# Float64 weights rebuilt as float32: which engine does which part of the bit work

## Chip, cores and metric

The kernel runs on one core of one Trainium2 chip. The metric is the device time of one execution in microseconds, median over runs. Times of single instructions, stages and waits come from one profiled execution.

## What is computed

Pooled attention over 4 batches and 8 heads (sequence 1152, head size 64), and behind it a rational MLP over the 2304 pooled rows. Cut to what matters:

```python
q_pool = q.reshape(B, H, S // 2, 2, D).mean(axis=3)
scores = q_pool @ k.transpose(0, 1, 3, 2) / np.sqrt(D)
attn = softmax(scores)                      # [4, 8, 576, 1152]
x = (attn @ v).transpose(0, 2, 1, 3).reshape(2304, 512)
h = x @ w_in                                # w_in [512, 2048], float64
P = a[0] + a[1]*h + a[2]*h**2 + a[3]*h**3
Q = 1 + abs(b[0])*abs(h) + abs(b[1])*h**2
out = (P / (Q + 1e-6)) @ w_out              # w_out [2048, 512], float64
```

The two weight matrices arrive as 64-bit floats. The chip's engines work on 32 bits, so the kernel has to make a float32 out of the two 32-bit words of every weight before it can use it.

## The kernel before

**Attention.** A unit is one batch and two heads. Preparing a unit loads k, q and v, pools q, takes a scale from sums of squares (ACT, L606), splits each operand in a high and a low float16 part (ACT L660 to L667, DVE L673 to L678), and turns k and q by transposing DMAs on SP's queue (L687). There are 144 attention tiles. A tile makes a first score product into the PSUM tile `sc` (L718), a row maximum on DVE (L725), a turn of it by a small matmul (L728) and a copy of that row by ACT (L732), a second score product into `st` (L741, L742), the exponential on ACT (L749) and a split of its result on DVE (L757). Products with v follow (L771), with a copy out by ACT (L788).

**MLP.** 18 chunks of 128 rows, 4 steps each. A step multiplies with `wi` (48 matmuls, L913) into one PSUM tile `ph`, runs a chain over ACT (L926, L931, L952, L956), DVE (L935, L939, L963, L967, L975) and POOL (L944, L948, L971), and multiplies with `wo` (12 matmuls, L984 to L986).

**Weights.** `wi` and `wo` are converted once, each in 16 pieces of 128 x 512 weights, in `weights` (L1092). A piece is loaded by SP (L457) into `raw`, which has two buffers and holds the low and the high word of each weight side by side, so that an engine that reads one of the words reads every second 32-bit word. `w_win` (L461) lets POOL read the high words as float32 and multiply them by 2^-111 into `wf`, which moves the exponent into the place it needs. `w_bits` (L467) is three DVE instructions: the top three bits of the low word are brought into the freed low half of the high word (L471, on 16-bit pieces), everything but the sign is cleared in the high word (L472), and `wf` is shifted left by 3 and joined with both by a bitwise or (L473). ACT then takes a sum of squares of the piece (`w_stat`, L478). When all 16 pieces are there, a scale is formed, ACT writes the high float16 part (L500) and DVE the low one (L504). For `wi`, column sums follow (L509 on ACT, L514, L517). `wo` uses the same `wf` buffer, so its first piece waits for the last low part of `wi`. The MLP's own tiles are opened by `w_close` (L524) once both weights are split: the first MLP step stands behind the last L504.

**What sets the order.** Each engine runs its instructions in a fixed order. `Plan` (L35) computes it when the kernel is built: every piece of work is added with an engine, a duration in ns and a due time, the planner goes forward and backward over them, and the earliest plan's order is written out for all engines. Those durations stand in the `add` calls (L1096 to L1099 for the weights); changing one can move any instruction of the program. At run time an instruction at the head of an engine's queue that waits holds all behind it on that engine.

## Time and profile before

| | |
|---|---|
| median of 3 runs | 953.59 us (952.13 to 958.34) |
| the profiled execution | 954.2 us, of which its span is 952.4 us |
| PE, DVE, ACT, POOL busy | 816.0, 794.1, 602.2, 446.0 us |
| first row maximum (L725) starts | 31.4 us |
| weight pieces of `wi`: first to last L473 starts | 12.7 to 113.1 us |
| weight pieces of `wo`: first to last L473 starts | 149.7 to 207.8 us |
| first MLP matmul (L913) | 232.7 us |
| PE busy up to 230 us, and behind it | 122.9 us of 230, 693.1 us of 722.4 |

How to read it: a busy share over the whole span mixes two stages. Up to 230 us there is attention and weight conversion and no MLP; behind it attention and MLP run side by side. A row of a group of instructions gives the line, the engine, what is written and read, the count, the busy time, the mean duration, and the idle time of the engine just before them with what ended it. The stretches table gives for each engine its busy time in a stretch, with the instruction count in brackets, and then the granted TensorE clock and the DMA share.

### The profile page before, as it was taken

The numbers are of one execution on the slowest core, as the hardware profiler recorded it, in microseconds if no ns is written. First come the engines' busy times: TensorE is split into PE (matmuls) and PEld (weight loads), VectorE is DVE, ScalarE is ACT, GpSimd is POOL, SyncE is SP. The second block draws the span as 40 slices with busy tenths as digits, with TensorE's granted clock in tenths as the row PEclk, the third lists the DMA queues.
The fourth block names the chain that finished last, engine by engine and source line by source line (L and its number), as shares of the span: only waits on it lengthen the run. The fifth ranks groups of instructions, "written<-read, shape, count | busy, mean of one in ns | idle before, by whom it ended". The sixth has DMA issues, their size and how long they took to land.

```text
span 952.4 us, 27847 instructions
## 1 busy us (share of the span) xinstructions
PE 816.0 (86%) x12196; PEld 650.4 (68%) x12196; DVE 794.1 (83%) x1075; ACT 602.2 (63%) x905; POOL 446.0 (47%) x482
## 2 busy tenths in 40 slices
PE   0477675545999999989998999989899998999998
PEld 0266554444877877768777788668677777887764
DVE  7698797888999897868999888869888897996765
ACT  4466595456876676657675686557667755775453
POOL 4212103342565553436764553425856544645765
PEclk9998777766999999979999999989999999999999
DMA  5784518462340060652150061445736120430100
GB/s 188 199 182 132 139 35 215 155 177 60 60 103 13 13 149 13 139 124 49 24 140 23 13 150 21 130 117 138 141 125 149 38 40 24 113 113 13 35 12 23
DMA packets 121338, 88.79 MB, mean 93 GB/s; under 512 B 96769, under 2 KB 98817, under 8 KB 121217
## 3 DMA queue, kind: packets, MB, share of 16 engines
q1 hardware_dynamic: 121216, 87.02, 37.0%
q8 instruction: 95, 1.56, 0.7%
q14 instruction: 27, 0.21, 0.1%
HBM read 49.24 MB, written 8.87 MB: 61 GB/s over the span
## 4 chain that ended last, share of the span: by engine, by line
PE 55%; DVE 12%; ACT 6%; POOL 6%; DMA 5%; issue 3%; SPq 1%; POOLq 0%; DVEq 0%; ACTq 0%
PE ph_h L913 15%; PE po L984 5%; PE po L986 5%; PE po L985 5%; PE st L741 5%; PE st L742 5%; PE sc L718 5%; PE sc L771 5%; PE st L771 4%; DVE mt L725 2%; DMA raw_wo<-in_moe_w_out_dram 2%; POOL e L944 1%; DMA k<-spk 1%; POOL e L948 1%; DVE E L757 1%
## 5 line engine op out<-in xcount | busy, mean ns | idle before, releaser
L749 ACT ACTIVATE E<-st,esc 128x1152 int32<-128x1152 f32 x144 | 188.6, 1310 | 92.4 <-PE st L728 63.0
L725 DVE TENSOR_REDUCE mt<-sc 128x1 f16<-128x1152 f32 x144 | 194.5, 1351 | 27.0 <-PE sc L718 18.9
L741 PE MATMUL st<-q,k 128*128 128x128 f16 (+1 forms) x1440 | 182.2, 224 | 34.9 <-ACT q L732 30.2
L913 PEld LDWEIGHTS <-wi 128*128 128x128 f16 x3456 | 199.9, 99 | 16.4 <-DVE t L939 9.3
L913 PE MATMUL ph_h<-x,wi 128*128 128x128 f16 x3312 | 201.9, 221 | 5.7 <-DVE t L939 5.7
L742 PE MATMUL st<-q,kb 65*128 65x128 f16 (+1 forms) x1440 | 182.7, 224 | 2.8 <-DMA kb<-k 2.8
L742 PEld LDWEIGHTS <-kb 65*128 65x128 f16 x1440 | 139.2, 103 | 49.0 <-issue 42.3
L971 POOL TENSOR_TENSOR e<-t,e 128x512 f32<-128x512 f32 x72 | 106.4, 1478 | 118.3 <-DVE e L967 108.4
L771 PEld LDWEIGHTS <-E 128*128 128x128 f16 (+1 forms) x4320 | 152.4, 105 | 12.9 <-issue 6.9
L757 DVE TENSOR_SCALAR E<-E 128x2304 f16<-128x2304 uint16 x144 | 129.8, 908 | 29.8 <-ACT E L749 29.6
L741 PEld LDWEIGHTS <-k 128*128 128x128 f16 x1440 | 139.7, 103 | 14.0 <-issue 8.8
L718 PE MATMUL sc<-k,q 128*128 128x384 f16 (+1 forms) x480 | 104.2, 354 | 42.3 <-DVE mt L725 25.6
L944 POOL TENSOR_SCALAR e<-A,b_abs 128x512 f32<-128x512 f32 x72 | 72.5, 1008 | 97.0 <-ACT A L926 97.0
L984 PE MATMUL po<-wo,g 128*128 128x512 f16 x288 | 109.2, 379 | 0.0
L986 PE MATMUL po<-wo,g 128*128 128x512 f16 x288 | 109.1, 379 | 0.0
L985 PE MATMUL po<-wo,g 128*128 128x512 f16 x288 | 109.1, 379 | 0.0
L948 POOL TENSOR_TENSOR e<-e,A 128x512 f32<-128x512 f32 x72 | 97.7, 1357 | 5.7
L718 PEld LDWEIGHTS <-q 128*128 128x128 f16 (+1 forms) x480 | 39.2, 104 | 69.2 <-issue 33.4
L952 ACT ACTIVATE A<-e,q_one 128x512 f32<-128x512 f32 x72 | 51.9, 721 | 51.7 <-POOL e L948 50.8
L926 ACT ACTIVATE A<-ph_h,cf 128x512 f32<-128x512 f32 x69 | 47.3, 686 | 58.2 <-PE ph_h L913 57.7
L975 DVE SCALAR_TENSOR_TENSOR g<-e,cf,A 128x512 f16<-128x512 f32 x72 | 63.0, 875 | 21.8 <-POOL e L971 21.7
L771 PE MATMUL sc<-v,E 128*128 128x65 f16 (+3 forms) x2160 | 80.3, 201 | 1.1 <-DVE mt L725 1.1
(126 smaller groups left out, 1212.6 us busy)
## 6 DMA issues: line engine op xcount, KB each, us to landing
kn<-in_k_dram SPq DMA_DIRECT2D x16, 576.0 KB, 4.2
vn<-in_v_dram SPq DMA_DIRECT2D x16, 576.0 KB, 5.4
qn<-in_q_dram SPq DMA_DIRECT2D x16, 512.0 KB, 4.9
raw_wi<-in_moe_w_in_dram SPq DMA_DIRECT2D x16, 512.0 KB, 5.3
raw_wo<-in_moe_w_out_dram SPq DMA_DIRECT2D x16, 512.0 KB, 3.6
kb<-k SPq DMA_DIRECT2D x18, 288.0 KB, 4.7
out_dram<-ob SPq DMA_DIRECT2D x16, 256.0 KB, 2.3
keep<-v SPq DMA_DIRECT2D x4, 292.5 KB, 6.2
```

The source lines that it names most:

```text
L718: nc.tensor.matmul(SC[ps, jj, 0:TH], d["q"][:, slot, ps], d["k"][:, h * KC + 3 * jj:h * KC + 3 * jj + 3, :].rearrange("p c m -> p (c m)"), ...
L725: nc.vector.tensor_reduce(mts[t % NM][:, D:D + 1], SC[:, :, 0:TH], AX.XY, ALU.max, negate=True)
L741: nc.tensor.matmul(o, d["k"][:, h * KC + c, :], d["q"][:, slot, qs], start=True, stop=False)
L742: nc.tensor.matmul(o, d["kb"][0:D + 1, h * KC + c, :], d["q"][0:D + 1, KC + slot, qs], start=False, stop=True)
L749: nc.scalar.activation(out=d["e"].rearrange("p (a c) -> p a c", a=3), in_=ST[:, :, 0:TH], func=AF.Exp, bias=esc[:, 1:2], scale=esc[:, 0:1],)
L757: nc.vector.tensor_scalar(e.bitcast(F16), e.bitcast(U16), 2.0 ** -6, None, ALU.mult)
L771: nc.tensor.matmul(pv[:, 0:w], e[:, c, qs, part], pairs[j][n_v][:, h * KC + c, :], start=(c == 0 and i == 0), stop=(c == KC - 1 and i == 2),)
L913: nc.tensor.matmul(mo[c, f]["p2"][:, i, :], wi[wl][:, kk, fs], x[:, xl * KD + kk, :], start=(n == 0), stop=(n == 3 * KD - 1))
L948: nc.gpsimd.tensor_tensor(w["e2"], w["e2"], w["A"], ALU.mult)
L984: nc.tensor.matmul(po, g[0][:, e, :], wo[0][:, kk, :], start=(kk == 0), stop=False)
L985: nc.tensor.matmul(po, g[0][:, e, :], wo[1][:, kk, :], start=False, stop=False)
L986: nc.tensor.matmul(po, g[1][:, e, :], wo[0][:, kk, :], start=False, stop=(kk == KF - 1))
```

## The change

`w_win` moves from POOL to ACT as a parametric relu with scale 2^-111 and a slope of -2^32 for negative inputs: a negative weight comes out positive with an exponent raised by 32, and that bit is the one that lands in the sign's place after the shift by 3. A new `w_low` lets POOL read the low words as 32-bit unsigned integers, multiply them by 2^-29 and 7.49/8 and write the result back as an integer from 0 to 7: these are the top three bits. `w_bits` keeps only the DVE instruction that shifts and joins, now with the low word. In the planner's table POOL's 700 becomes ACT's 630, POOL gets 830 for `w_low`, and DVE's 2300 becomes 800. Behind the changed lines, line numbers are higher by two.

```diff
     def w_win(n, i):
...
-        u = st["raw", n, i][:, :, 1]
-        nc.gpsimd.tensor_scalar(st["wf", n][:, i, :], u.bitcast(F32), 2.0 ** -111, 1.0, ALU.mult, ALU.mult)
+        u = st["raw", n, i][:, :, 1].bitcast(F32)
+        nc.scalar.activation(out=st["wf", n][:, i, :], in_=u, func=AF.Prelu, scale=2.0 ** -111, alpha=-(2.0 ** 32))
+
+    def w_low(n, i):
+        u = st["raw", n, i][:, :, 0].bitcast(U32)
+        nc.gpsimd.tensor_scalar(u, u, 2.0 ** -29, 7.49 / 8, ALU.mult, ALU.mult)

     def w_bits(n, i):
         mi = st["wf", n][:, i, :].bitcast(I32)
-        r = st["raw", n, i]
-        h = r.rearrange("p f w -> p (f w)").bitcast(U16).rearrange("p (f w) -> p f w", w=4)
-        nc.vector.tensor_scalar(h[:, :, 2], h[:, :, 1], 13, None, ALU.logical_shift_right)
-        nc.vector.tensor_scalar(h[:, :, 3], h[:, :, 3], 0x8000, None, ALU.bitwise_and)
-        nc.vector.scalar_tensor_tensor(mi, mi, 3, r[:, :, 1], ALU.logical_shift_left, ALU.bitwise_or)
+        nc.vector.scalar_tensor_tensor(mi, mi, 3, st["raw", n, i][:, :, 0], ALU.logical_shift_left, ALU.bitwise_or)
...
-            add("pool", 700, s + 4, lambda i=i: w_win(n, i), r=[raw], w=[wf], seq=["win"])
-            add("dve", 2300, s + 4, lambda i=i: w_bits(n, i), w=[wf, raw])
+            add("act", 630, s + 4, lambda i=i: w_win(n, i), r=[raw], w=[wf], seq=["win"])
+            add("pool", 830, s + 4, lambda i=i: w_low(n, i), w=[(*raw, "low")], r=[raw], seq=["low"])
+            add("dve", 800, s + 4, lambda i=i: w_bits(n, i), r=[raw, (*raw, "low")], w=[wf])
```

The planner's new order moves instructions on all engines. Three places matter below.

DVE near the start of the program, before the change: the bit work of the second and third piece of `wi`, around the first unit's scale (L618, L622) and its low parts (L678, L675).

```order
L471 TENSOR_SCALAR raw_wi_153<-raw_wi_153 128x512
L472 TENSOR_SCALAR raw_wi_153<-raw_wi_153 128x512
L473 SCALAR_TENSOR_TENSOR wf_wi<-wf_wi,raw_wi_153 128x512
L618 SCALAR_TENSOR_TENSOR pp_186<-sc,sc_102 128x4
L622 RECIPROCAL ss_187<-pp_186 128x4
L471 TENSOR_SCALAR raw_wi_176<-raw_wi_176 128x512
L472 TENSOR_SCALAR raw_wi_176<-raw_wi_176 128x512
L473 SCALAR_TENSOR_TENSOR wf_wi<-wf_wi,raw_wi_176 128x512
L678 SCALAR_TENSOR_TENSOR spk_158<-kn_140,ss_187,spk_158 128x18x64
L675 SCALAR_TENSOR_TENSOR spq<-qn_145,ss_187,spq 128x9x64
```

The same place in the changed kernel (L475 is the joining instruction, L680 and L677 the low parts).

```order
L475 SCALAR_TENSOR_TENSOR wf_wi<-wf_wi,raw_wi_153 128x512
L620 SCALAR_TENSOR_TENSOR pp_184<-sc,sc_102 128x4
L624 RECIPROCAL ss_185<-pp_184 128x4
L680 SCALAR_TENSOR_TENSOR spk_158<-kn_140,ss_185,spk_158 128x18x64
L677 SCALAR_TENSOR_TENSOR spq<-qn_145,ss_185,spq 128x9x64
```

The first unit's low parts now stand directly behind its scale; the third piece of weights went behind them.

ACT in the conversion of `wo`, before the change: sums of squares (L478) among exponentials (L749) and the small row copies (L732).

```order
L478 ACTIVATE wo_91,wst_wo<-wf_wo 128x512
L749 ACTIVATE E_1920<-st,esc_953 128x1152
L788 ACTIVATE xf_0_604<-st 128x130
L478 ACTIVATE wo_91,wst_wo<-wf_wo 128x512
L732 ACTIVATE q_1122<-st 1x128
L478 ACTIVATE wo_91,wst_wo<-wf_wo 128x512
L749 ACTIVATE E_2020<-st,esc_953 128x1152
L478 ACTIVATE wo_91,wst_wo<-wf_wo 128x512
```

The same stage in the changed kernel. L467 is the parametric relu, which reads what a load has just brought; L480 is the sum of squares, L751 the exponential, L734 the row copy.

```order
L751 ACTIVATE E_1903<-st,esc_879 128x1152
L467 ACTIVATE wf_wo<-raw_wo_1887 128x512
L480 ACTIVATE wo_91,wst_wo<-wf_wo 128x512
L467 ACTIVATE wf_wo<-raw_wo_1899 128x512
L480 ACTIVATE wo_91,wst_wo<-wf_wo 128x512
L734 ACTIVATE q_1120<-st 1x128
L790 ACTIVATE xf_0_702<-st 128x130
L751 ACTIVATE E_1949<-st,esc_879 128x1152
```

Each piece now has two instructions on ACT, and the first of them waits for a DMA on the queue that also carries the exponentials.

DVE in the conversion of `wo`, before the change: row maxima (L725) and splits (L757) among the three instructions of each piece.

```order
L725 TENSOR_REDUCE mt_103<-sc 128x1
L471 TENSOR_SCALAR raw_wo_1890<-raw_wo_1890 128x512
L472 TENSOR_SCALAR raw_wo_1890<-raw_wo_1890 128x512
L473 SCALAR_TENSOR_TENSOR wf_wo<-wf_wo,raw_wo_1890 128x512
L757 TENSOR_SCALAR E_1920<-E_1920 128x2304
L471 TENSOR_SCALAR raw_wo_1928<-raw_wo_1928 128x512
L472 TENSOR_SCALAR raw_wo_1928<-raw_wo_1928 128x512
L473 SCALAR_TENSOR_TENSOR wf_wo<-wf_wo,raw_wo_1928 128x512
```

The same stage in the changed kernel (L727 is the row maximum, L759 the split).

```order
L727 TENSOR_REDUCE mt_104<-sc 128x1
L475 SCALAR_TENSOR_TENSOR wf_wo<-wf_wo,raw_wo_1939 128x512
L759 TENSOR_SCALAR E_1949<-E_1949 128x2304
L475 SCALAR_TENSOR_TENSOR wf_wo<-wf_wo,raw_wo_1954 128x512
L680 SCALAR_TENSOR_TENSOR spk_1693<-kn_1483,ss_1961,spk_1693 128x18x64
L677 SCALAR_TENSOR_TENSOR spq<-qn_1623,ss_1961,spq 128x9x64
L727 TENSOR_REDUCE mt_105<-sc 128x1
```

One instruction of a piece stands between the work of attention where three stood, and the 16 pieces of `wo` are spread over more row maxima: 13 where there were 6.

Counted on PE, 32 turns of a row maximum (L728) stand ahead of the first MLP matmul (L913) before the change, and 41 (L730) ahead of it (L915) in the changed kernel. At the tenth MLP step the two orders meet: 47 turns stand ahead of its first matmul in both.

More of the change, by code (lines that the diff above doesn't have):

```diff
@@ L13 @@
 U16 = mybir.dt.uint16
+U32 = mybir.dt.uint32
 BF16 = mybir.dt.bfloat16
```

## Prediction

> **What bounds the kernel now.** I read the page's head first, then the table of stretches, because the busy shares of the whole span mix two stages.
>
> ```profile
> span 952.4 us, 27847 instructions
> PE 816.0 (86%) x12196; PEld 650.4 (68%) x12196; DVE 794.1 (83%) x1075; ACT 602.2 (63%) x905; POOL 446.0 (47%) x482
> ```
>
> PE looks like the bound, with DVE three points behind. The stretches part them. Behind a stretch's bounds and length stand the busy us of PE, PE's weight loads, DVE, ACT and POOL (instructions in brackets), the granted clock, the DMA share and GB/s.
>
> ```profile
> 10.00:31.00 21.00, 1.25 (x5) 0.61 (x6) 15.80 (x26) 7.76 (x17) 8.82 (x10) 1.00 0.63 149
> 31.00:115.00 84.00, 57.70 (x818) 47.04 (x816) 67.23 (x92) 49.92 (x85) 17.88 (x24) 0.88 0.66 169
> 115.00:147.00 32.00, 22.34 (x255) 16.64 (x256) 27.75 (x42) 28.81 (x30) 1.11 (x6) 0.79 0.25 66
> 147.00:209.00 62.00, 32.13 (x465) 27.12 (x464) 52.30 (x79) 30.89 (x61) 26.98 (x34) 0.70 0.59 174
> 209.00:230.00 21.00, 9.47 (x91) 7.22 (x92) 20.04 (x29) 14.00 (x20) 4.72 (x8) 0.50 0.42 103
> 230.00:307.00 77.00, 74.32 (x1241) 62.90 (x1239) 73.52 (x88) 54.00 (x80) 41.03 (x36) 0.98 0.27 58
> 307.00:952.40 645.40, 618.80 (x9329) 488.81 (x9326) 532.17 (x709) 412.61 (x611) 343.08 (x359) 0.98 0.32 76
> ```
>
> From 230 us on PE is busy for 74.3 + 618.8 of 722.4 us, 96%: that stage is bound by PE. Before it PE is nearly idle by comparison, and DVE is busy for 15.8 + 67.2 + 27.8 + 52.3 + 20.0 = 183.1 of the 220 us from 10 to 230, 83%, against 131.4 us (60%) of ACT and 59.5 us of POOL. So the head of the program goes by DVE. The groups of instructions on DVE from 10 to 230 us say what it does there.
>
> ```profile
> L725 DVE TENSOR_REDUCE mt<-sc 128x1 f16<-128x1152 f32 x33 | 44.5, 1349 | 6.6 <-PE sc L718 5.1 <-PE sc L771 1.3
> L757 DVE TENSOR_SCALAR E<-E 128x2304 f16<-128x2304 uint16 x29 | 23.8, 824 | 10.7 <-ACT E L749 10.7
> L472 DVE TENSOR_SCALAR raw_wi<-raw_wi 128x512 uint16<-128x512 uint16 x16 | 13.0, 814 | 0.0
> L472 DVE TENSOR_SCALAR raw_wo<-raw_wo 128x512 uint16<-128x512 uint16 x16 | 12.8, 799 | 0.0
> L473 DVE SCALAR_TENSOR_TENSOR wf_wo<-wf_wo,raw_wo 128x512 int32<-128x512 int32 x16 | 12.3, 769 | 0.6
> L471 DVE TENSOR_SCALAR raw_wi<-raw_wi 128x512 uint16<-128x512 uint16 x16 | 12.2, 765 | 5.4 <-POOL wf_wi L465 5.4
> L471 DVE TENSOR_SCALAR raw_wo<-raw_wo 128x512 uint16<-128x512 uint16 x16 | 11.9, 746 | 4.5 <-POOL wf_wo L465 4.5
> L473 DVE SCALAR_TENSOR_TENSOR wf_wi<-wf_wi,raw_wi 128x512 int32<-128x512 int32 x16 | 11.4, 711 | 0.6
> ```
>
> The bit work is 73.6 us of DVE's 183.1, and its idle columns are short: DVE's queue is seldom empty.
>
> **The change, part by part.** The two 16-bit instructions go: 13.0 + 12.8 + 12.2 + 11.9 = 49.9 us of DVE, which becomes 133.2 us. The joining instruction stays as it is, with a low word in place of a high one, at the same step through memory. ACT's rows of the head price what comes in.
>
> ```profile
> L749 ACT ACTIVATE E<-st,esc 128x1152 int32<-128x1152 f32 x30 | 39.2, 1308 | 29.9 <-PE st L728 19.4 <-PE st L771 5.3 <-PE st L742 5.0
> L478 ACT ACTIVATE wo<-wf_wo 128x512 f16<-128x512 f32 x16 | 10.0, 628 | 15.0 <-DVE wf_wo L473 14.9
> L478 ACT ACTIVATE wi<-wf_wi 128x512 f16<-128x512 f32 x16 | 10.0, 625 | 15.4 <-DVE wf_wi L473 15.3
> L732 ACT ACTIVATE q<-st 1x128 f16<-1x128 f32 x31 | 8.3, 268 | 2.3 <-PE st L728 1.7
> ```
>
> A parametric relu over 128x512 is nearest to L478 (same shape, 625 to 628 ns); I take 0.63 us, so 32 of them add 20.2 us. Its bounds are 0.63, since it does no less, and 0.69, the 128x512 form that reads `ph_h` in L926 below: 2 us over 32 pieces, nothing.
>
> POOL swaps one product for another.
>
> ```profile
> L465 POOL TENSOR_SCALAR wf_wi<-raw_wi x16: 632/718/1254, 10.1 to 109.7; 128x512 f32<-128x512 f32 x16
> ```
>
> ```profile
> L971 POOL TENSOR_TENSOR e<-t,e 128x512 f32<-128x512 f32 x72 | 106.4, 1478 | 118.3 <-DVE e L967 108.4
> ```
>
> The new one converts from and to integers and also writes with a step, which no row shows. From below it costs the 0.63 us of the fastest copy, from above the 1.48 us of POOL's dearest 128x512 instruction, L971; I take 0.8, near the median, because L465 is the nearest in shape and step. POOL's 59.5 of 220 us leave room, so only its latency counts: it runs beside the relu, and DVE waits for the later one. At 1.48 us a piece is 0.7 us later, and with two buffers that is up to 32 x 0.7 / 2 = 11 us, if nothing hides it.
>
> Moved work: the new order puts 41 attention tiles ahead of the first MLP step, not 32. Nine tiles more cost DVE 9 x (1.35 + 0.82) = 19.6 us and ACT 9 x (1.31 + 0.27) = 14.2 us; the units prepared there are as many as before (five). So for the head DVE stands at 152.8 us and **ACT at 131.4 + 20.2 + 14.2 = 165.8 us**. ACT becomes the fuller engine. If it reaches the 83% that DVE reaches now, the head takes 10 + 165.8 / 0.83 = 210 us.
>
> It will not quite, because of the wait that moves. From the table of waits: engine and line, what released it, us in total, times, the longest.
>
> ```profile
> POOL wf_wi L465 <- DMA raw_wi<-in_moe_w_in_dram: 40.3, 13, 6.7
> POOL wf_wo L465 <- DMA raw_wo<-in_moe_w_out_dram: 30.7, 12, 6.7
> DVE raw_wi L471 <- POOL wf_wi L465: 5.4, 5, 1.8
> DVE raw_wo L471 <- POOL wf_wo L465: 4.5, 7, 1.2
> ```
>
> POOL waits 71.0 us for landing weights, which costs nothing, as nothing else there is urgent. DVE, one step behind in its own queue, sees 9.9 us of that lateness. Now ACT waits for the same landings, and queued behind the relu are exponentials, row copies and sums of squares; PE's second score product waits for the row copies, DVE's split for the exponentials. The bounds are nothing and 71 us. I take a quarter, 18 us, nearer to DVE's 9.9: the relus stand in the order among other work, as DVE's instructions did, while POOL had nothing else to do and stood waiting early. The sums of squares keep their waits of 30.4 us (15.0 and 15.4 in L478's rows) or shorten them, as the way through DVE gets shorter; I count no gain. So the point that lies at 230 us now, where the first MLP step is due, comes at **S = 228 us**, with nine tiles more done.
>
> At the start there is a small gain inside that sum. The first unit's k is split behind three pieces' bit work, and its transpose behind that.
>
> ```profile
> 19.37 0.69 DVE L473 SCALAR_TENSOR_TENSOR wf_wi<-wf_wi,raw_wi 128x512 int32<-128x512 int32 x1
> 19.98 1.41 DVE L678 SCALAR_TENSOR_TENSOR spk<-kn,ss,spk 128x1152 f16<-128x1152 f32 x1
> 31.36 1.36 DVE L725 TENSOR_REDUCE mt<-sc 128x1 f16<-128x1152 f32 x1 [2.43 <-PE sc L718]
> ```
>
> The third piece's 2.2 us and the waits around it leave that path, and the first row maximum should start near 26 us, not 31.4.
>
> A rule of the Trainium skill speaks against the part that stays on DVE. L473 has a longest copy far above its median.
>
> ```profile
> L473 DVE SCALAR_TENSOR_TENSOR wf_wo<-wf_wo,raw_wo x16: 691/693/1623, 149.7 to 207.8; 128x512 int32<-128x512 int32 x16
> ```
>
> The mean is 0.77 us, so long copies are rare: 16 x 0.08 = 1.3 us for `wo`. The Trainium skill (GPSIMD Engine Reference, 8. Key points) says that GpSimd shares its SBUF interfaces with VectorE and contends with DVE instructions that have two SBUF inputs, which L473 has. The rare long copies agree with it; by the rule alone every joining instruction that meets a product would be one of them. It is a rival below.
>
> **What the nine tiles are worth.** After S the two orders have to reach the same point: the tenth MLP step with 47 tiles behind it. Now that stretch is bound by PE.
>
> ```profile
> L913 PE MATMUL ph_h<-x,wi 128*128 128x128 f16 x432 | 26.1, 219 | 0.0
> L984 PE MATMUL po<-wo,g 128*128 128x512 f16 x18 | 6.8, 379 | 0.0
> L728 PE MATMUL st<-ident,mt 128*128 128x128 f16 x15 | 3.4, 226 | 1.3 <-DVE mt L725 1.3
> ```
>
> ```profile
> 250.90 2.68 PE ph_h L913 x48
> ```
>
> ```profile
> 314.13 0.69 ACT L926 ACTIVATE A<-ph_h,cf 128x512 f32<-128x512 f32 x1 [1.11 <-PE ph_h L913]
> ```
>
> From 230 to 307 us PE ran 9 steps' 48 matmuls, at 2.68 us a step (the chain's row) 24.1 us; 54 output matmuls (18 in each of three lines), which are four times as wide, so 54 x 4 x 2.68 / 48 = 12.1 us; and 15 tiles in what is left of 74.3: 2.54 us a tile. The tenth step's ACT work starts at 314.1, so the stretch is 84.1 us now, and without nine tiles 84.1 - 9 x 2.54 = 61.2 us. The steps' own pace allows that: at the end of the program, where hardly any attention is left, this row has four intervals in 25.5 us, 6.4 each, and nine steps take 57 us.
>
> ```profile
> L926 ACT ACTIVATE A<-ph_h,cf x5: 687/687/688, 898.0 to 923.5; 128x512 f32<-128x512 f32 x5
> ```
>
> **The sum.** The meeting point comes at 228 + 61.2 = 289.2 and not 314.1 us, 24.9 us earlier. From there on both have the same work in nearly the same order, bound by PE, and I expect it to take as long. The span becomes 927.5; the profiled execution had 1.8 us around its span (954.2 against 952.4) and was 0.6 above the median of the three runs (953.59), so the time is 929 us. About 1%, 9.5 us, is what a measurement of this kernel can tell from no change.
>
> **Rivals.** First, the landings' wait takes ACT over (slower). Relus at the head of ACT's queue hold the exponentials. For it: ACT has the most work, and the loads land late against many a wait of POOL's (25 of 32). Against it: DVE saw little of that. From a wait of 314.1 - 61.2 - 210 = 43 us on nothing is gained; at 60 us S is 270 and the time 971 us.
>
> Second, the steps pace the stretch after S, and the nine tiles buy little. In the changed order five steps stand within one tile, so PE has only their matmuls, and a step's chain on ACT, DVE and POOL must turn faster than it does now. At 8.6 us a step, halfway between the last intervals here (7.4 from 306.7 to 314.1, 9.8 to the next), nine take 77 us, the meeting is at 305 and the time 945 us: within 1%.
>
> ```profile
> 306.70 0.69 ACT L926 ACTIVATE A<-ph_h,cf 128x512 f32<-128x512 f32 x1 [1.56 <-PE ph_h L913]
> 323.93 0.69 ACT L926 ACTIVATE A<-ph_h,cf 128x512 f32<-128x512 f32 x1 [1.26 <-PE ph_h L913]
> ```
>
> Third, ACT hides the landings altogether, since half its queue does not depend on them: S is 210, the time 911 us. For it: at 165.8 us in 200 ACT still has a sixth of its time idle to take waits in. Against it: DVE, which was fuller and stood a step further back, still saw 9.9 us.
>
> Fourth, each joining instruction meets a POOL product and takes 1.62 us, as the longest did: 32 x 0.93 = 30 us more, DVE at 183 us, the fuller engine again, S = 10 + 183 / 0.83 + 18 = 248 and the time 949 us. Against it: 1.3 us of excess in 16 copies now. The Trainium skill's rule on the shared interfaces, above, is the one that would have it so.
>
> Fifth, the relu is not free of table loads. One load is in the trace.
>
> ```profile
> L417 ACT ACT_TABLE_LOAD x1 | 1.3, 1283 | 0.7 <-PEq L1249 0.7
> ```
>
> If each of 32 relus forced one before it and one behind it, ACT would gain 64 x 1.28 = 82 us, S would be 327 and the time 1028 us. Against it: the changed program has one such load on ACT's list, as before. The Trainium skill (ScalarE: Activation LUTs, Table sets: the hidden batching unit) says that functions are loaded as sets, that cheap ones like relu are in every set, and that changing the set costs a load; the parametric form is not named there.
>
> **How the numbers follow.** Chances: the forecast (918 to 941) 0.57, ACT hides all (911) 0.14, the steps' pace (945) 0.13, the port (949) 0.05, the landings (971) 0.10, tables 0.01. Faster by over 1% takes the first two and a third of the pace case, 0.75; slower by over 1% the last two and little else, 0.11; the rest, 0.14, is within 1%. The range goes from 909, below the case without waits, to 953, above the pace and port cases, and leaves out the landings' case and the tables. POOL's 11 us lie in it.
>
> **What would show it.** Right: no 16-bit instruction on DVE, the joining one at 0.69 to 0.77 us; relus at 0.63; DVE at 70 to 75% and ACT at 75 to 80% from 10 us to the first MLP matmul, which starts between 215 and 240 us; ACT's wait for landing weights between 5 and 35 us; the first row maximum near 26 us; the tenth step near 289. Wrong: an ACT wait for `raw` over 43 us, a POOL product over 1.5 us, a first MLP matmul behind 253 us, or a tenth step that comes early and an end that does not, which would mean that the stage behind it is not bound by PE's work alone.

## The result and the profile after

| | before | changed |
|---|---|---|
| median | 952.86 us (4 runs, 950.86 to 958.34) | 927.78 us (4 runs, 926.45 to 929.13) |
| ratio | | 0.9728, 95% interval 0.9683 to 0.9773 |
| span of the profiled execution | 952.4 us | 924.7 us |
| first MLP matmul | 232.7 us | 211.4 us |
| ACT work of the first MLP step | 235.64 us | 215.94 us |
| ACT work of the tenth MLP step | 314.13 us | 286.81 us |

The time came out 1 us from the forecast. The way there is another one than was forecast, and the last two rows of the table show it first: they cut the span into the head (up to the first step), the stretch (first to tenth step) and the rest. "Head" also names the part from 10 us to the first MLP matmul, for which the stretches table gives busy times.

The head of the changed kernel's page:

```profile
span 924.7 us, 27851 instructions
PE 809.6 (88%) x12196; PEld 640.1 (69%) x12196; DVE 750.5 (81%) x1011; ACT 620.5 (67%) x937; POOL 445.4 (48%) x482
```

DVE lost 64 instructions and 43.6 us, ACT gained 32 and 18.3 us. The stretches table of the changed kernel (bounds and length, then PE, weight loads, DVE, ACT, POOL, clock, DMA share, GB/s): the head from 10 us to the first MLP matmul, and the stretch from the first step's ACT work to the tenth's.

```profile
10.00:211.00 201.00, 125.29 (x1758) 97.67 (x1758) 153.30 (x217) 155.03 (x255) 58.48 (x81) 0.84 0.62 162
215.94:286.81 70.87, 68.23 (x1153) 57.90 (x1152) 63.66 (x82) 53.15 (x74) 45.87 (x37) 1.00 0.28 59
```

The same two of the kernel before, cut at its own points:

```profile
10.00:232.00 222.00, 124.89 (x1648) 100.36 (x1649) 184.78 (x266) 131.71 (x211) 59.51 (x80) 0.79 0.56 147
235.64:314.13 78.49, 75.81 (x1263) 63.89 (x1262) 75.71 (x90) 57.62 (x85) 44.09 (x39) 1.00 0.27 57
```

In the head DVE went from 83% to 76% and ACT from 59% to 77%: they are now level. The stretch is bound by PE in both (97% and 96%) and shorter by the PE time that left it: 75.81 - 68.23 = 7.6 us, 110 matmuls. From the tenth step to the end it is 638.3 us before and 924.7 - 286.81 = 637.9 now. So of the 27.7 us of span **19.7 are the head, 7.6 the stretch, 0.4 the rest**.

What the engines do in the head. The changed kernel's groups on DVE from 10 to 211 us:

```profile
L727 DVE TENSOR_REDUCE mt<-sc 128x1 f16<-128x1152 f32 x41 | 55.5, 1354 | 16.9 <-PE sc L720 12.5 <-PE sc L358 1.6 <-PE sc L773 1.5
L759 DVE TENSOR_SCALAR E<-E 128x2304 f16<-128x2304 uint16 x32 | 26.6, 835 | 7.4 <-ACT E L751 7.4
L475 DVE SCALAR_TENSOR_TENSOR wf_wi<-wf_wi,raw_wi 128x512 int32<-128x512 int32 x16 | 11.7, 743 | 5.3 <-POOL raw_wi L471 2.3 <-ACT wf_wi L467 1.5 <-issue 1.5
L475 DVE SCALAR_TENSOR_TENSOR wf_wo<-wf_wo,raw_wo 128x512 int32<-128x512 int32 x16 | 11.0, 687 | 6.7 <-POOL raw_wo L471 6.5
```

On ACT in the same 201 us:

```profile
L751 ACT ACTIVATE E<-st,esc 128x1152 int32<-128x1152 f32 x32 | 41.9, 1310 | 9.0 <-PE st L730 5.2 <-PE st L773 2.8 <-PE st L744 0.4
L734 ACT ACTIVATE q<-st 1x128 f16<-1x128 f32 x41 | 11.0, 268 | 11.5 <-PE st L730 9.4 <-PE st L744 1.4
L467 ACT ACTIVATE wf_wo<-raw_wo 128x512 f32<-128x512 f32 x16 | 10.6, 670 | 4.5 <-DMA raw_wo<-in_moe_w_out_dram 4.4
L467 ACT ACTIVATE wf_wi<-raw_wi 128x512 f32<-128x512 f32 x16 | 10.5, 668 | 3.0 <-DMA raw_wi<-in_moe_w_in_dram 2.9
L480 ACT ACTIVATE wi<-wf_wi 128x512 f16<-128x512 f32 x16 | 10.0, 624 | 3.9 <-DVE wf_wi L475 3.8
L480 ACT ACTIVATE wo<-wf_wo 128x512 f16<-128x512 f32 x16 | 9.9, 621 | 1.2 <-DVE wf_wo L475 1.2
```

Read the counts first: 41 row maxima and 41 row copies, but only 32 exponentials and 32 splits. Then the last column: ACT waits 4.4 + 2.9 = 7.3 us for landing weights, and its sums of squares (L480) wait 3.8 + 1.2 = 5.0 us for DVE, where they waited 30.2 us.

The waits of the changed kernel up to 211 us (who waits, for what, us in total, times, longest):

```profile
POOL raw_wi L471 <- DMA raw_wi<-in_moe_w_in_dram: 28.6, 13, 7.9
POOL raw_wo L471 <- DMA raw_wo<-in_moe_w_out_dram: 20.1, 9, 4.7
DVE wf_wo L475 <- POOL raw_wo L471: 6.5, 7, 2.0
DVE wf_wi L475 <- POOL raw_wi L471: 2.3, 2, 1.9
```

POOL still stands 48.7 us in wait for the loads, and DVE sees 8.8 us of it, where it saw 9.9.

### The profile page after: what moved, and what is told of

Same layout as the page of the kernel before. It is cut to its first block, busy times and chain, and to the rows that moved or that the text cites. A ratio compares the mean times of both kernels' runs of the same rounds, so it can differ in the third digit from the quotient of the medians.

```text
span 924.7 us, 27851 instructions
## 1 busy us (share of the span) xinstructions
PE 809.6 (88%) x12196; PEld 640.1 (69%) x12196; DVE 750.5 (81%) x1011; ACT 620.5 (67%) x937; POOL 445.4 (48%) x482
## 4 chain that ended last, share of the span: by engine, by line
PE 54%; DVE 17%; ACT 11%; DMA 6%; issue 5%; POOL 4%; SPq 2%; POOLq 0%; DVEq 0%; ACTq 0%
PE ph_h L915 14%; PE st L743 6%; PE st L744 6%; PE sc L773 6%; PE st L773 5%; PE sc L720 5%; PE po L986 4%; PE po L988 4%; PE po L987 4%; ACT E L751 4%; DVE mt L727 3%; DVE E L759 2%; DVE t L941 2%; DVE g L965 2%; DVE t L937 2%
## 5 line engine op out<-in xcount | busy, mean ns | idle before, releaser
L751 ACT ACTIVATE E<-st,esc 128x1152 int32<-128x1152 f32 x144 | 188.6, 1310 | 68.3 <-PE st L730 45.7
L727 DVE TENSOR_REDUCE mt<-sc 128x1 f16<-128x1152 f32 x144 | 194.8, 1353 | 43.9 <-PE sc L720 32.5
L915 PEld LDWEIGHTS <-wi 128*128 128x128 f16 x3456 | 199.6, 99 | 24.2 <-DVE t L941 15.8
L915 PE MATMUL ph_h<-x,wi 128*128 128x128 f16 x3312 | 201.6, 221 | 10.5 <-DVE t L941 8.6
L743 PE MATMUL st<-q,k 128*128 128x128 f16 (+1 forms) x1440 | 179.4, 222 | 17.6 <-ACT q L734 12.2
L744 PE MATMUL st<-q,kb 65*128 65x128 f16 (+1 forms) x1440 | 179.8, 222 | 2.5 <-DMA kb<-k 2.5
L973 POOL TENSOR_TENSOR e<-t,e 128x512 f32<-128x512 f32 x72 | 111.4, 1547 | 141.3 <-DVE e L969 118.7
L773 PEld LDWEIGHTS <-E 128*128 128x128 f16 (+1 forms) x4320 | 146.9, 103 | 11.5 <-issue 7.1
L743 PEld LDWEIGHTS <-k 128*128 128x128 f16 x1440 | 137.7, 102 | 17.2 <-issue 12.3
L759 DVE TENSOR_SCALAR E<-E 128x2304 f16<-128x2304 uint16 x144 | 126.8, 883 | 27.4 <-ACT E L751 27.2
L720 PE MATMUL sc<-k,q 128*128 128x384 f16 (+1 forms) x480 | 104.2, 353 | 41.2 <-DVE mt L727 28.6
L720 PEld LDWEIGHTS <-q 128*128 128x128 f16 (+1 forms) x480 | 40.4, 105 | 73.7 <-issue 44.4
L928 ACT ACTIVATE A<-ph_h,cf 128x512 f32<-128x512 f32 x69 | 47.3, 685 | 58.5 <-PE ph_h L915 56.0
L977 DVE SCALAR_TENSOR_TENSOR g<-e,cf,A 128x512 f16<-128x512 f32 x72 | 64.9, 901 | 21.4 <-POOL e L973 21.3
L773 PE MATMUL sc<-v,E 128*128 128x65 f16 (+3 forms) x2160 | 77.3, 198 | 0.0
```

The source lines that it names most:

```text
L720: nc.tensor.matmul(SC[ps, jj, 0:TH], d["q"][:, slot, ps], d["k"][:, h * KC + 3 * jj:h * KC + 3 * jj + 3, :].rearrange("p c m -> p (c m)"), ...
L727: nc.vector.tensor_reduce(mts[t % NM][:, D:D + 1], SC[:, :, 0:TH], AX.XY, ALU.max, negate=True)
L743: nc.tensor.matmul(o, d["k"][:, h * KC + c, :], d["q"][:, slot, qs], start=True, stop=False)
L744: nc.tensor.matmul(o, d["kb"][0:D + 1, h * KC + c, :], d["q"][0:D + 1, KC + slot, qs], start=False, stop=True)
L751: nc.scalar.activation(out=d["e"].rearrange("p (a c) -> p a c", a=3), in_=ST[:, :, 0:TH], func=AF.Exp, bias=esc[:, 1:2], scale=esc[:, 0:1],)
L759: nc.vector.tensor_scalar(e.bitcast(F16), e.bitcast(U16), 2.0 ** -6, None, ALU.mult)
```

## Experiments

Time is compared by the ratio to the kernel before, timed on the same chip beside it; a difference of 0.01 is 9.5 us. Of every kernel the table gives the start of ACT's work of the first and of the tenth MLP step, in its one profiled execution. x2, x3, x4, x7 and x11 have the changed kernel's order, so their last column should be its 637.9 us too; it goes up to 642.4. A part of a span is therefore known to some 4 us only.

| kernel | ratio, 95% interval | first step, us | first to tenth | tenth to end |
|---|---|---|---|---|
| before | 1 | 235.6 | 78.5 | 638.3 |
| changed | 0.9728 (0.9683 to 0.9773) | 215.9 | 70.9 | 637.9 |
| x1_new_ops_old_order | 0.9916 (0.9899 to 0.9932) | 229.5 | 78.4 | 638.1 |
| x2_old_ops_new_order | 0.9967 (0.9943 to 0.9991) | 237.4 | 70.9 | 638.3 |
| x3_relu_on_pool | 0.9794 (0.9760 to 0.9828) | 221.7 | 70.9 | 642.4 |
| x4_relu_twice | 0.9870 (0.9853 to 0.9888) | 229.4 | 70.9 | 640.6 |
| x7_dve_padded | 0.9908 (0.9888 to 0.9928) | 233.9 | 70.8 | 637.8 |
| x11_dve_pad_ahead | 0.9909 (0.9875 to 0.9944) | 235.1 | 71.0 | 639.8 |
| x5_four_buffers | 0.9638 (0.9609 to 0.9667) | 197.6 | 76.9 | 641.4 |
| x8_four_buffers_padded | 0.9822 (0.9796 to 0.9847) | 211.3 | 76.9 | 645.0 |
| x6_measured_costs | 0.9841 (0.9817 to 0.9865) | 219.3 | 75.5 | 642.7 |
| x9_before_measured_costs | 0.9869 (0.9840 to 0.9899) | 227.4 | 77.8 | 635.1 |
| x10_after_costs_shifted | 0.9729 (0.9699 to 0.9760) | 218.7 | 69.5 | 638.2 |

### The new instructions in the old order

The planner gets its old costs, so that every engine keeps the old order, and POOL's old place issues both the relu and the POOL product.

```diff
-            add("act", 630, s + 4, lambda i=i: w_win(n, i), r=[raw], w=[wf], seq=["win"])
-            add("pool", 830, s + 4, lambda i=i: w_low(n, i), w=[(*raw, "low")], r=[raw], seq=["low"])
-            add("dve", 800, s + 4, lambda i=i: w_bits(n, i), r=[raw, (*raw, "low")], w=[wf])
+            add("pool", 700, s + 4, lambda i=i: (w_win(n, i), w_low(n, i)), r=[raw], w=[wf], seq=["win"])
+            add("dve", 2300, s + 4, lambda i=i: w_bits(n, i), w=[wf, raw])
```

> The changed kernel's instructions in the order of the kernel before: the planner gets the old costs, and each relu is issued on ACT where POOL's product stands. Theory one (the gain is DVE's 50 us of head time; the new order adds only first score products ahead of the MLP): the first MLP matmul stays near 211 us, the stretch to the tenth step is 78 us as before, and the time is 930 to 940 us. Rival (the new order brought the gain): the first MLP matmul comes behind 225 us and the time is 945 us or more. If ACT's wait for landing weights matters, it shows here, since the relus stand where POOL waited 71 us: over 30 us of wait on ACT and a late MLP.

Its head in the stretches table:

```profile
10.00:226.00 216.00, 126.23 (x1649) 101.88 (x1649) 140.36 (x202) 150.25 (x243) 50.04 (x80) 0.79 0.57 151
```

947.76 us, 0.8% under before: in the old order the lighter DVE brings the first step only 6.1 us forward and nothing in the stretch. DVE is at 65% and ACT at 70%, so neither is full here. The rival's time came; that the order by itself brought the gain is what the next run asks. ACT's waits for landing weights, up to 232 us:

```profile
ACT wf_wo L467 <- DMA raw_wo<-in_moe_w_out_dram: 7.1, 8, 1.5
ACT wf_wi L467 <- DMA raw_wi<-in_moe_w_in_dram: 6.1, 4, 2.1
```

13.2 us, not over 30. But from 10 us on, the chain of work that ended last passes in this head through six landings of weight pieces, 32.5 us, where that of the kernel before has three, 16.7 us, and that of the changed kernel four, 15.8 us. That points to the loads and their two buffers, but weakly: the chain of x10 below, as fast as the changed kernel, has none in its head. It is not shown: no run gives the old order more buffers.

### The old instructions in the new order

Here the planner keeps the changed kernel's costs, POOL's plain product stands at the place of the new POOL product, the relu's place is empty, and DVE has its three instructions again (`w_win` and `w_bits` are those of the kernel before, left out of the cut).

```diff
-            add("act", 630, s + 4, lambda i=i: w_win(n, i), r=[raw], w=[wf], seq=["win"])
-            add("pool", 830, s + 4, lambda i=i: w_low(n, i), w=[(*raw, "low")], r=[raw], seq=["low"])
+            add("act", 630, s + 4, lambda i=i: None, r=[raw], w=[wf], seq=["win"])
+            add("pool", 830, s + 4, lambda i=i: w_win(n, i), w=[(*raw, "low")], r=[raw], seq=["low"])
```

> The instructions of the kernel before (product on POOL, three on DVE) in the changed kernel's order. Theory one: DVE carries 50 us more than in the changed kernel's head, so the first MLP matmul comes at 240 to 255 us and the time is 952 to 970 us. Rival (the order is what pays): about 930 us.

Its head, and the first and the tenth step in its timeline:

```profile
10.00:232.00 222.00, 132.25 (x1758) 103.11 (x1758) 196.26 (x281) 137.07 (x223) 63.05 (x81) 0.80 0.56 147
```

```profile
237.37 0.69 ACT L928 ACTIVATE A<-ph_h,cf 128x512 f32<-128x512 f32 x1 [5.70 <-PE ph_h L915]
308.23 0.69 ACT L928 ACTIVATE A<-ph_h,cf 128x512 f32<-128x512 f32 x1 [1.03 <-PE ph_h L915]
```

950.96 us, next to nothing: 1 us under the theory's range and far from the rival's 930. The first MLP matmul, at 232.3 us, came ahead of the 240 to 255 given. The stretch is 70.9 us, the changed kernel's to a tenth, and the head is as long as before, with DVE at 88%. So the stretch goes by the order alone, and the order alone pays for its shorter stretch with more row maxima in DVE's head (196.3 us of DVE against 184.8). **Instructions alone bring 8 us of 953, the order alone 3, both 26.** In the new order the instructions are worth 23 us, in the old one 8.

### DVE's two instructions put back

The changed kernel, in its own order, with the two 16-bit instructions of before issued again, behind the joining one, where nothing of the weights' path waits for their result.

```diff
         nc.vector.scalar_tensor_tensor(mi, mi, 3, st["raw", n, i][:, :, 0], ALU.logical_shift_left, ALU.bitwise_or)
+        h = st["raw", n, i].rearrange("p f w -> p (f w)").bitcast(U16).rearrange("p (f w) -> p f w", w=4)
+        nc.vector.tensor_scalar(h[:, :, 2], h[:, :, 1], 13, None, ALU.logical_shift_right)
+        nc.vector.tensor_scalar(h[:, :, 3], h[:, :, 3], 0x8000, None, ALU.bitwise_and)
```

> The changed kernel with the two 16-bit DVE instructions of before put behind each joining instruction, on words that nothing reads any more: 50 us more on DVE in the head, ACT and POOL as changed, same order. If DVE's time is what the change bought, the first MLP matmul comes at 235 us or later and the time is 950 to 965 us. If it was the shorter way from landing to sum of squares that paid, and not DVE's time, under 940 us.

```profile
10.00:229.00 219.00, 133.71 (x1758) 104.12 (x1758) 189.78 (x281) 155.83 (x253) 64.78 (x81) 0.79 0.55 149
```

944.28 us, 17 us more than the changed kernel (0.9908 - 0.9728 = 0.018), all of it in the head. DVE is at 87% (83% before the change). Neither number of the expectation held: it is between them.

The same two put ahead of the joining instruction, behind the relu, so that they also lengthen the way to the sum of squares:

```diff
+        h = st["raw", n, i].rearrange("p f w -> p (f w)").bitcast(U16).rearrange("p (f w) -> p f w", w=4)
+        nc.vector.tensor_scalar(h[:, :, 2], h[:, :, 1], 13, None, ALU.logical_shift_right)
+        nc.vector.tensor_scalar(h[:, :, 3], h[:, :, 3], 0x8000, None, ALU.bitwise_and)
         nc.vector.scalar_tensor_tensor(mi, mi, 3, st["raw", n, i][:, :, 0], ALU.logical_shift_left, ALU.bitwise_or)
```

> As the padded run with two buffers, but the two 16-bit DVE instructions stand ahead of the joining one, behind the relu: the same work on every engine, and 1.5 us more between landing and sum of squares. The padded run took 944 us. If the way through a piece counts beside DVE's time, ACT waits over 20 us at its sums of squares (5.0 in the changed kernel) and the time is 950 to 965 us; if only DVE's busy time counts, 942 to 948 us.

```profile
10.00:231.00 221.00, 135.78 (x1758) 105.52 (x1758) 191.14 (x281) 156.11 (x255) 64.55 (x81) 0.78 0.55 148
```

Its waits of ACT's sums of squares for DVE:

```profile
ACT wi L483 <- DVE wf_wi L478: 10.1, 6, 2.8
ACT wo L483 <- DVE wf_wo L478: 7.1, 8, 2.4
```

946.6 us, ratio 0.9909 against 0.9908. ACT waits 17.2 us there, against 7.8 with the two behind, and the time is the same. So what these instructions cost comes from the time that they take on DVE, and not from the longer path of a piece. They could also cost by holding a piece's buffer longer; the run with four buffers below asks that.

### The relu twice, and the relu on POOL

One asks what a microsecond on ACT costs, the other what ACT's part is worth. In the first, line 467 stands twice. In the second the relu is replaced by POOL's old product of the high words, which leaves out the sign of the weights.

```diff
+        nc.scalar.activation(out=st["wf", n][:, i, :], in_=u, func=AF.Prelu, scale=2.0 ** -111, alpha=-(2.0 ** 32))
```

> The changed kernel with every relu issued twice, the second with the same input and output: 32 x 0.67 = 21 us more on ACT, same order. If ACT has room in the head: 927 to 934 us. If ACT bounds the head: 21 us divided by an 80% share, 945 us or more.

```profile
10.00:224.00 214.00, 133.73 (x1758) 103.61 (x1758) 152.74 (x217) 175.41 (x287) 53.84 (x81) 0.78 0.57 152
```

943.18 us: some 20 us more on ACT (175.4 against 155.0) cost 13.5 us (0.9870 - 0.9728), in the head. It is between the two ranges, nearer to the one in which ACT is the bound. ACT is at 82%, DVE at 71%. So ACT's relu is not under cover of DVE's work. The second relu also stands between the landing of a piece and its joining instruction; what of the 13.5 us is ACT's time and what this longer path was not separated.

```diff
-        u = st["raw", n, i][:, :, 1].bitcast(F32)
-        nc.scalar.activation(out=st["wf", n][:, i, :], in_=u, func=AF.Prelu, scale=2.0 ** -111, alpha=-(2.0 ** 32))
+        u = st["raw", n, i][:, :, 1]
+        nc.gpsimd.tensor_scalar(st["wf", n][:, i, :], u.bitcast(F32), 2.0 ** -111, 1.0, ALU.mult, ALU.mult)
```

> The changed kernel with ACT's relu put back to POOL as the old plain product, so POOL has two products a piece and ACT none; the sign of the weights is left out. Same order. If ACT is the fuller engine of the head, as the prediction had it, 21 us less on ACT bring the MLP 10 us or more earlier: 910 to 918 us. If DVE and the waits between engines set the head and ACT has room, the time stays at 924 to 932 us.

```profile
10.00:217.00 207.00, 129.67 (x1758) 101.00 (x1758) 155.34 (x217) 136.37 (x223) 82.27 (x113) 0.82 0.59 158
```

```profile
ACT wo L480 <- DVE wf_wo L475: 11.2, 8, 3.0
ACT wi L480 <- DVE wf_wi L475: 10.0, 5, 4.1
DVE wf_wo L475 <- POOL wf_wo L467: 8.6, 7, 2.2
DVE wf_wi L475 <- POOL wf_wi L467: 7.0, 6, 2.5
DVE wf_wo L475 <- POOL raw_wo L471: 5.2, 6, 1.3
DVE wf_wi L475 <- POOL raw_wi L471: 3.7, 2, 2.0
```

937.26 us, slower than the changed kernel by 6 us in ratio (0.9794 against 0.9728; the intervals overlap slightly), and outside both ranges of the expectation. POOL is at 40% of its time and still costs: with both products one behind the other on POOL, DVE waits 8.6 + 7.0 + 5.2 + 3.7 = 24.5 us for it, and ACT 21.2 us for DVE. The change puts the two on two engines side by side, which speaks for the shorter waits of ACT as a part of its gain, one for which the prediction counted nothing.

### Four buffers for the landing pieces

The loads' part was open: POOL's wait for landings is long in every kernel, and two `raw` buffers limit how early a load may start. The pieces now land in four slices of the second `wo` tile, which is not yet in use then.

```diff
-        t = st["stg"].tile([P, 512, 2], I32, tag="raw", name=f"raw_{n}{i}", bufs=NRAW)
+        b = 4 * (i % 4)
+        t = wo[1][:, b:b + 4, :].rearrange("p c f -> p (c f)").bitcast(I32).rearrange("p (f w) -> p f w", w=2)
...
-            raw, wf = ("raw", i % NRAW), ("wf", i)
+            raw, wf = ("raw4", i % 4), ("wf", i)
```

> The changed kernel with four buffers for landed pieces in place of two (they lie where the low part of the output weights is written later), which the planner uses; its order has 33 turns ahead of the MLP, not 41. If the head waits for loads and for the two buffers, the first MLP matmul comes at 190 to 200 us and the time is 910 to 922 us, though the stretch behind it is some 7 us longer again. If the engines' own work and order set the head, the first MLP matmul stays within 208 to 215 us and the time is 928 to 938 us.

```profile
10.00:194.00 184.00, 121.43 (x1671) 97.92 (x1671) 143.29 (x201) 149.43 (x241) 50.69 (x80) 0.85 0.67 177
```

**918.13 us, the best of all, 3.6% under before** and 8.6 us under the changed kernel (0.9728 - 0.9638). The head is 18.4 us shorter, and its order takes only 33 turns ahead, so that the stretch is 6.1 us longer. Of the 18.4 some are those maxima: DVE has 10 us less to do there, ACT 5.6. The last joining instruction of `wi` starts at 71.8 us, not 95.4, and ACT is at 81%, DVE at 78%: both wait less. Time and first MLP matmul (194.5 us) are in the ranges expected if the two buffers hold the head back, beside ACT and DVE. That they do is not shown by this run alone, since the planner's order changes along with the buffers, and the last group of runs shows what orders can do.

With DVE's two instructions put back in this kernel, behind the joining one:

```diff
+        h = st["raw", n, i].rearrange("p f w -> p (f w)").bitcast(U16).rearrange("p (f w) -> p f w", w=4)
+        nc.vector.tensor_scalar(h[:, :, 2], h[:, :, 1], 13, None, ALU.logical_shift_right)
+        nc.vector.tensor_scalar(h[:, :, 3], h[:, :, 3], 0x8000, None, ALU.bitwise_and)
```

> Four buffers, and the two 16-bit DVE instructions put behind each joining one as in the padded run with two. With four buffers a later release of a buffer delays no load, so the difference to the unpadded run with four is DVE's time alone: 15 us or more if DVE's queue sets the head, under 6 us if the padded run with two buffers lost its time through the buffers.

```profile
10.00:208.00 198.00, 118.26 (x1671) 95.61 (x1671) 181.80 (x265) 151.07 (x243) 67.15 (x80) 0.85 0.62 164
```

935.58 us, 17.5 us more (0.9822 - 0.9638), and DVE is at 92%. Only 13.7 us of it lie in the head (211.3 against 197.6), where it was 17.9 with two buffers; 3.6 us lie behind the tenth step, where no weights are converted. Either way it is far over the 6 us expected if the two cost mainly by holding a buffer longer: most of their price is DVE's time. That it is the same with four buffers as with two holds for the whole time and is not shown for the head.

### Other costs in the planner's table

If so much hangs on the order, how much of it is luck? The changed kernel's three durations are replaced by values near the medians of its profile, and in another run shifted by 10 ns each; and the kernel before gets its measured ones. No instruction changes, only their order.

```diff
-            add("act", 630, s + 4, lambda i=i: w_win(n, i), r=[raw], w=[wf], seq=["win"])
-            add("pool", 830, s + 4, lambda i=i: w_low(n, i), w=[(*raw, "low")], r=[raw], seq=["low"])
-            add("dve", 800, s + 4, lambda i=i: w_bits(n, i), r=[raw, (*raw, "low")], w=[wf])
+            add("act", 670, s + 4, lambda i=i: w_win(n, i), r=[raw], w=[wf], seq=["win"])
+            add("pool", 670, s + 4, lambda i=i: w_low(n, i), w=[(*raw, "low")], r=[raw], seq=["low"])
+            add("dve", 690, s + 4, lambda i=i: w_bits(n, i), r=[raw, (*raw, "low")], w=[wf])
```

> The changed kernel with the planner's durations for the three parts set to what the trace shows (ACT 670, POOL 670, DVE 690 in place of 630, 830, 800). The order moves a little (40 turns ahead of the MLP). Theory: the head is a chain of queues, so an order nearer to the truth gives a few us, 920 to 928; rival: nothing but scatter, 926 to 932.

937.81 us: with durations nearer to the truth the same instructions are 11 us slower (0.9841 - 0.9728), some 3 us of it in the head, 5 in the stretch and 5 behind it. Both theories missed.

The kernel before, with durations near its own profile's:

```diff
-            add("pool", 700, s + 4, lambda i=i: w_win(n, i), r=[raw], w=[wf], seq=["win"])
-            add("dve", 2300, s + 4, lambda i=i: w_bits(n, i), w=[wf, raw])
+            add("pool", 670, s + 4, lambda i=i: w_win(n, i), r=[raw], w=[wf], seq=["win"])
+            add("dve", 2210, s + 4, lambda i=i: w_bits(n, i), w=[wf, raw])
```

> The kernel before with the planner's durations for the weights set to the trace's (POOL 670, DVE 2210 in place of 700, 2300): nothing but the order moves. It says how far an order scatters. If the change's gain is the work and not a lucky order, 945 to 962 us; if orders alone scatter by as much as the gain, below 940 us or above 965.

```profile
10.00:222.00 212.00, 124.69 (x1649) 100.13 (x1649) 179.57 (x261) 129.12 (x205) 58.62 (x79) 0.80 0.53 138
```

942.25 us: the old instructions, in another order, are 12.5 us faster than before. That is under the range for a gain that comes from the work alone, and nearly half of the change's 26 us.

The changed kernel, each duration moved by 10 ns:

```diff
-            add("act", 630, s + 4, lambda i=i: w_win(n, i), r=[raw], w=[wf], seq=["win"])
-            add("pool", 830, s + 4, lambda i=i: w_low(n, i), w=[(*raw, "low")], r=[raw], seq=["low"])
-            add("dve", 800, s + 4, lambda i=i: w_bits(n, i), r=[raw, (*raw, "low")], w=[wf])
+            add("act", 640, s + 4, lambda i=i: w_win(n, i), r=[raw], w=[wf], seq=["win"])
+            add("pool", 820, s + 4, lambda i=i: w_low(n, i), w=[(*raw, "low")], r=[raw], seq=["low"])
+            add("dve", 790, s + 4, lambda i=i: w_bits(n, i), r=[raw, (*raw, "low")], w=[wf])
```

> The changed kernel with the planner's durations shifted by 10 ns each (ACT 640, POOL 820, DVE 790): the same instructions in another order. With the measured durations the same kernel took 938 us. If an order scatters by about 10 us, anything from 920 to 940 us; the gain is the work's if it stays below 942 us.

929.29 us, as expected within 920 to 940; the ratio, 0.9729, is the changed kernel's own. Its first step is 2.7 us later and its stretch 1.3 us shorter.

So the old instructions have run in three orders, at 953, 951 and 942 us, and the new ones in the changed kernel's three tables at 928, 929 and 938, and in the old order at 948. The best of the old stands 3 us in ratio behind the worst of the new tables (0.9869 against 0.9841, the intervals overlap) and ahead of the new ones in the old order (0.9916), while orders move each by some 10. The gain of 26 us can't be cut into a fixed part of the instructions and one of the order. What is measured at an unchanged order is the price of DVE's two instructions: 17 us with two buffers, in both places (x7 and x11), and 17.5 with four.

## Why the prediction came out right, step by step

**That the head goes by the fuller of DVE and ACT: held, with a limit.** Where DVE carries its two instructions again it stands at 86 to 92% (x2, x7, x8, x11; 83% before the change), without them ACT and DVE are level in the changed kernel, and work added to either costs. The limit is x1: 65% and 70%, and a head that is hardly shorter. There the order or the loads pace it; the chain points to the loads, and it stays open.

**ACT at 165.8 us: 11 us too much.** The step that failed is "Nine tiles more cost DVE 9 x (1.35 + 0.82) = 19.6 us and ACT 9 x (1.31 + 0.27) = 14.2 us". It counted turns of row maxima and took each for a tile. The groups of the head above show what was moved: 41 maxima and 41 row copies, where the prediction's rows of before have 33 and 31, but only 32 exponentials and 32 splits, where those have 30 and 29. What went ahead of the first MLP step is the first half of nine tiles. The runs price it: with the old instructions in both orders (the kernel before and x2) the new order adds 137.07 - 131.71 = 5.4 us to ACT's head, not 14.2, and 196.26 - 184.78 = 11.5 to DVE's, not 19.6. In the new order the relus add 155.03 - 137.07 = 18.0 us (from x2 to the changed kernel), forecast 20.2.

**DVE at 152.8 us: the number held by luck.** The trace has 153.3. But the nine tiles were 8 us too dear, and the "49.9 us of DVE" that go were 7 us too many: from x2 to the changed kernel DVE loses 196.26 - 153.30 = 43.0 us. The forecast added up durations, and these overlap. In the kernel before:

```profile
174.07 0.74 DVE L471 TENSOR_SCALAR raw_wo<-raw_wo 128x512 uint16<-128x512 uint16 x1
174.61 0.77 DVE L472 TENSOR_SCALAR raw_wo<-raw_wo 128x512 uint16<-128x512 uint16 x1
```

The second starts 0.54 us after the first, which takes 0.74.

**The 18 us of ACT's waits for landings: too much; 7.3 us**, inside the band of 5 to 35 that was given. And "I count no gain" for the sums of squares missed 25 us of waiting that went: 30.2 us before, 5.0 now. One joining instruction stands where three instructions stood between POOL's product and the sum of squares. How much of the 25 us was worth time is not settled; in x1 these waits fell to 3.4 us as well and the head was only 6 us shorter, and between the two padded kernels 9.4 us of such waiting (17.2 against 7.8) cost nothing while DVE was the fuller engine.

So S was put 18 us too late. The point that stood at 230 us moved, as the first step's work did, by 19.7 us, and came at about 210 us and not 228. The prediction's own formula with the measured terms, 10 + 155.0 / 0.83 + 7.3, gives 204, 6 us under that; ACT reached only 155.0 / (210 - 10 - 7.3) = 80% beside its landing waits. So of the 18 us, 13 come from ACT's miscounted work (10.8 / 0.83) and 11 from its landing waits, and the lower share takes 6 back. S = 210 is also what the third rival had, but not by its mechanism: the landings' wait is small, not hidden, and ACT is not at 165.8 us.

**The stretch: the same error with the other sign.** "9 x 2.54" took 22.9 us off it. It lost 7.6. PE's groups from the first step's ACT work to the tenth's, in the changed kernel (215.94 to 286.81 us):

```profile
L743 PE MATMUL st<-q,k 128*128 128x128 f16 (+1 forms) x153 | 17.5, 213 | 0.7 <-ACT E L751 0.7
L773 PE MATMUL sc<-v,E 128*128 128x65 f16 x162 | 5.4, 193 | 0.0
L720 PE MATMUL sc<-k,q 128*128 128x384 f16 (+1 forms) x22 | 4.3, 328 | 0.3 <-DVE mt L727 0.3
L730 PE MATMUL st<-ident,mt 128*128 128x128 f16 x7 | 1.5, 219 | 0.0
```

and in the kernel before (235.64 to 314.13 us):

```profile
L741 PE MATMUL st<-q,k 128*128 128x128 f16 (+1 forms) x162 | 18.7, 213 | 1.1 <-ACT q L732 1.1
L771 PE MATMUL sc<-v,E 128*128 128x65 f16 (+1 forms) x216 | 7.2, 193 | 0.3 <-DVE mt L725 0.3
L718 PE MATMUL sc<-k,q 128*128 128x384 f16 (+1 forms) x47 | 9.0, 328 | 0.0
L728 PE MATMUL st<-ident,mt 128*128 128x128 f16 x15 | 3.3, 220 | 1.3 <-DVE mt L725 1.3
```

First products (L718, L720) fell from 47 to 22 and turns from 15 to 7, but second products only from 162 to 153 in each of their two lines, and products with v by one group of 54 (L771 and L773, written to `sc`). So nine whole tiles never stood ahead.

So S was 18 us late and the stretch 15 us too short in the forecast; the meeting point, forecast at 289.2, came at 286.8. **The time was right by luck: the two errors nearly cancelled, and one miscount, of turns taken for tiles, stands behind the whole of the second and a good half of the first.** The size of the whole, the place of the gain (ahead of the tenth step) and the bound behind it (637.9 us against 638.3) were right; the division was not.

**The smaller terms.** The relu took 0.668 to 0.670 us, forecast 0.63 and at most 0.69. The POOL product's mean was 0.80 and 0.89 us, forecast 0.8; one copy of 32 took 1.70 us, over the 1.5 that was named as a sign of being wrong, but the mean did not follow. The first MLP matmul came at 211.4 us, ahead of the 215 to 240 that was given. The first row maximum starts near its forecast of 26 us. The changed kernel's timeline on DVE:

```profile
14.87 1.42 DVE L680 SCALAR_TENSOR_TENSOR spk<-kn,ss,spk 128x1152 f16<-128x1152 f32 x1 [1.65 <-ACT spk L669]
25.06 1.36 DVE L727 TENSOR_REDUCE mt<-sc 128x1 f16<-128x1152 f32 x1 [4.31 <-PE sc L720]
```

**The rivals.** The landings' wait (7.3 us against the 43 from which it decides) and the port did not come. All copies of the joining instruction in the changed kernel (min, median and max in ns):

```profile
L475 DVE SCALAR_TENSOR_TENSOR wf_wi<-wf_wi,raw_wi x16: 676/684/1179, 11.0 to 95.4; 128x512 int32<-128x512 int32 x16
L475 DVE SCALAR_TENSOR_TENSOR wf_wo<-wf_wo,raw_wo x16: 669/693/703, 131.8 to 186.5; 128x512 int32<-128x512 int32 x16
```

None reaches 1.62 us. Their means above, 0.743 and 0.687 us, are 0.06 over and 0.01 under the medians, so long copies cost 1 us in all 32. Where the two did meet in the changed kernel, POOL had the longer time:

```profile
140.68 0.68 DVE L475 SCALAR_TENSOR_TENSOR wf_wo<-wf_wo,raw_wo 128x512 int32<-128x512 int32 x1
140.72 1.15 POOL L471 TENSOR_SCALAR raw_wo<-raw_wo 128x512 uint32<-128x512 uint32 x1 [0.58 <-ACT wo L480]
```

Three POOL products began 0.04 to 0.11 us behind the start of a joining instruction; they took 1.09, 1.15 and 1.13 us against a median of 0.67, and the joining instructions 0.67 to 0.69. Three products that ran wholly beside a row maximum took 0.64 to 0.66. So the trace agrees with the contention in the Trainium skill's rule (GPSIMD Engine Reference, 8. Key points). But the longer time fell on POOL, which is busy for 58.5 of the 201 us of the head, and not on every joining instruction, as the rival had it. The table loads did not come either:

```profile
L418 ACT ACT_TABLE_LOAD x1 | 1.3, 1283 | 0.7 <-PEq L1252 0.7
```

One load, with 32 parametric relus standing among exponentials and sums of squares. That the steps' pace decides in the stretch did not come: PE is busy for 68.23 of its 70.87 us.

## What to carry to other kernels

When an order moves work ahead of a stage, count every kind of instruction that is moved: a turn that stands earlier is not a tile that stands earlier, and one miscount enters two terms with opposite signs, so check the point where the stages meet and not only the end. Price the relief of an engine by its busy time, not by summed durations, which can overlap, and at an unchanged order (put the removed instructions back as padding), and vary the planner's table by a few tens of ns before an edit is credited with a per cent. After a relief look at once for the next thing that holds the stage: here four landing buffers instead of two, with the order that came of them, brought another 9 us.

## What was unexpected in the hardware

The POOL product that converts from and to 32-bit integers and writes every second word in place is no dearer than the plain float product it replaced: median 677 and 665 ns, where the old one's were 718 and 664 ns (single copies reach 1.70 us, the old one's 1.25). The changed kernel's rows:

```profile
L471 POOL TENSOR_SCALAR raw_wi<-raw_wi x16: 644/677/1699, 9.9 to 92.7; 128x512 uint32<-128x512 uint32 x16
L471 POOL TENSOR_SCALAR raw_wo<-raw_wo x16: 643/665/1182, 130.8 to 185.3; 128x512 uint32<-128x512 uint32 x16
```

The parametric relu, which reads every second word, took 668 and 670 ns, some 45 more than the sum of squares over the same count of contiguous elements (624 and 621 ns); whether the function, the step through memory or the wider output (float32, not float16) costs it was not separated.
